# A diffusion transformer block on one core: a first chunk of four tiles of scale features, a new order of the head, and half tiles of the scores in pairs

## The chip, the core and the metric

The kernel runs on one core of one Trainium2 chip. The core has a matrix engine (TensorE, in the profile PE for its matmuls and PEld for its weight loads), a vector engine (DVE), a scalar engine (ACT), a general one (POOL) and a queue engine (SP) that issues most transfers. Matmuls take their operands from the on-chip memory SBUF (128 partitions) and write to PSUM, an accumulator memory of eight banks, each of 512 columns in float32 on 128 partitions. DVE and ACT read PSUM and write SBUF. The engines run their own instruction streams and wait for each other through semaphores.

The metric is the time of one execution in microseconds (us), as the device measures it; lower is better.

## What is computed

`x` holds two images (B = 2) of 256 tokens with 1152 features; `c` is one conditioning vector for each image. Everything is bfloat16 at the boundary.

```python
B, N, D = (2, 256, 1152); F = 4 * D
H = 2; Dh = D // H
mod = (_silu(c) @ w_mod).reshape(B, 6, 1, D)
shift_a, scale_a, gate_a, shift_m, scale_m, gate_m = [mod[:, i] for i in range(6)]
h = _layernorm(x, axis=-1) * (1 + scale_a) + shift_a
qkv = (h @ wqkv).reshape(B, N, 3, H, Dh)
q, k, v = qkv[:, :, 0], qkv[:, :, 1], qkv[:, :, 2]
attn = _softmax(jnp.einsum('bqhd,bkhd->bhqk', q, k) * Dh ** (-0.5), axis=-1)
a = jnp.einsum('bhqk,bkhd->bqhd', attn, v).reshape(B, N, D) @ wo
x = x + gate_a * a
h2 = _layernorm(x, axis=-1) * (1 + scale_m) + shift_m
m = _gelu(h2 @ w_fc1) @ w_fc2
return x + gate_m * m
```

1152 features are nine tiles of 128. A head has 576 features, which is four and a half tiles; so the fifth tile of Q (index 4) and of K (index 13 in the common buffer) belongs with its partitions 0 to 63 to head 0 and with its partitions 64 to 127 to head 1.

## The kernel before

**Planner.** The kernel records its work as units on the five engines, with the memory regions that each instruction reads and writes; a list scheduler then fixes an order for every engine and puts in the semaphore waits. TensorE and SP keep the order in which the units are recorded. DVE and ACT start with a list written out by hand (`S.first`) and go on by priority. Dependences in SBUF are by byte ranges. In PSUM they are by bank: an instruction of DVE or ACT waits for the last matmul of every TensorE unit that wrote the bank, for earlier accesses to the same bank by the other of the two engines, and a TensorE unit that writes a bank anew waits for all that read it before.

**Head.** The first transfers are `c` (issued from ACT), then, on SP's queue in this order: the two images of `x`; the scale columns of `w_mod` for the first `KC` = 5 feature tiles, in three pieces of three row blocks each (`ld_sc0_*`, WSC); the K weights of row blocks 0 to 4 (WK); the scale columns of the last four tiles in three pieces; the K weights of row blocks 5 to 8; the shift columns (WSH). Later come the Q weights (WQ), which use the place of WSC and whose loads wait until TensorE has read the row block of WSC that they overwrite.

While these arrive, TensorE runs matmuls without use (`warm`, identity times zeros `Q4B`, 512 columns) and turns `c` by a transpose. The layer norm's statistics of the four token tiles are shared between DVE (tiles 1 and 2: `bn_*`, `aggr_*`, `veps_*`) and ACT (tiles 0 and 3: `sq_*`, `sum_*`, then `nvar_*`, `veps_*` on DVE); POOL takes the inverse root, DVE writes the normalised tile `xn_t`. `xn_T(t)` transposes a token tile in nine matmuls of 128 columns into banks 4, 5, 6 for image 0 and 6, 4, 5 for image 1 (`XB`): feature tiles 0 to 3 in the first of these banks, 4 to 7 in the second, 8 in the third. `mod_kt` makes the scale features with matmuls of two columns into bank 7; `sc1a` (line 783, DVE) adds 1.

`hk(kt, b)` (line 792 on DVE, line 790 on ACT) multiplies feature tile `kt` of image `b` by its scale and writes it to `HK`. For the tiles of the first chunk it reads the transposed tile straight from PSUM; the others are first copied to SBUF by ACT (`xn_T_copy`, line 681), and scaled from there when the second chunk of scale features is known.

K is accumulated in pairs of output tiles (`k_pair`), each in one bank: image 0 in banks 0 to 3, image 1 in banks 5, 4, 6 (its fourth pair comes later, in bank 1). A pair takes two matmuls of 256 columns for each feature tile. Before, TensorE's order is: 15 warming matmuls, `xn_T(1)`, piece 0 of the scale features, one warming matmul, `xn_T(0)`, piece 1, two warming ones, piece 2, three warming ones; then the first five feature tiles of K of image 0 with `xn_T(2)` and `xn_T(3)` after the second and third of them; the first pair of image 1 with five tiles; all of the second chunk of scale features (36 matmuls); the second and third pair of image 1; and then the remaining feature tiles for both images. The contribution of the shift to K is left out, as it adds the same to all scores of a query, and shift is added (`hx`) only for Q and V.

**Q and scores.** Six tiles of Q are accumulated side by side in six banks, then moved to `QK` by ACT and DVE in turn (`qk_evac`). Tiles 6, 7 and 8 follow one by one (`proj`). `s_and_softmax(b, h)` computes the scores of one image and head, two blocks of 128 queries by 256 keys side by side in one bank (`s_bank`), over five chunks of features (`head_chunks`). The shared fifth tile of Q is stored twice: `QK[:, 4]` with zeros in partitions 64 to 127 (memset `z4a`) for head 0, and `Q4B` with zeros in partitions 0 to 63 for head 1. So both heads take a full matmul of 128 rows for it. DVE takes the row maximum, ACT the exponentials, DVE normalises. Between the scores stand the V projections; then come the transposed probabilities, the modulation rows, attention times V, the output projection, the second layer norm and the MLP, none of which the diff touches.

Where four small matmuls fill the four column groups of the array (`quad_mm`, for shift and for the modulation rows), a `tile_position` names the place; in the kernel before that is the only use of it.

Of the kernel before, what the change touches and what calls it, by code (L numbers as in the profile page):

```python
# [500 lines left out]
KT = 9  # L501
# [5 lines left out]
CH = 384  # L507
NCH = 3
F0 = 8
KC = 5  # L510
KG = 6


def c_mm(n):
    return max(n / 2.4 + 2.5, 27.0)
# [26 lines left out]
def build_kernel(nc, x, c, wqkv, wo, w_mod, w_fc1, w_fc2, out):  # L542
    S = Sched()
# [4 lines left out]
    with (  # L548
# [42 lines left out]
        WQ = wmat(O_A, D)  # L591
# [78 lines left out]
        def dve(cost, fn, reads, writes, name):  # L670
            return S.op("dve", cost, fn, reads=reads, writes=writes, name=name)
# [88 lines left out]
        def xn_T(t):  # L760
            b = t // 2
            S.unit("pe", KT * c_mm(128), "xnT_%d" % t)
            for kt in range(KT):
                tr(ps16(XB[b][kt // 4], (kt % 4) * 256 + (t % 2) * 128, 128), XN[:, t, kt * 128:(kt + 1) * 128], IDENT)

        def xn_T_copy(b, k0, k1, eng):
            src = ps16(XB[b][k0 // 4], (k0 % 4) * 256, (k1 - k0) * 256).rearrange("p (k t) -> p k t", k=k1 - k0)
            copy_on(eng, HX[:, k0:k1, b * 256:(b + 1) * 256], src, (k1 - k0) * 256, True, "xnT_cp%d_%d" % (b, k0))

        def warm(n, tag):  # L770
            for i in range(n):
                S.unit("pe", 215.0, "warm_%s_%d" % (tag, i))
                mm(ps32(2), IDENT, Q4B, True, True)

        def mod_kt(W, kt, col0, name, fs=(0, 9)):
            S.unit("pe", (fs[1] - fs[0]) * 27.0, name)
            for f in range(*fs):
                mm(ps32(7, col0 + f * 2, 2), W[:, kt, f * 128:(f + 1) * 128], ST[:, kt:18:9], kt == 0 and f == fs[0], kt == KT - 1,
                   skip_group_check=True)
# [6 lines left out]
        def hk(kt, b, eng="dve"):  # L786
            dst, s1 = HK[:, kt, b * 256:(b + 1) * 256], SC1A[:, kt * 2 + b:kt * 2 + b + 1]
            src = ps16(XB[b][kt // 4], (kt % 4) * 256, 256) if kt < KC else HX[:, kt, b * 256:(b + 1) * 256]
            if eng == "act":
                act(c_act(256, 1), lambda e: e.activation(out=dst, in_=src, func=ACTF.Copy, scale=s1), [src, s1], [dst], "hk_%d_%d" % (kt, b))  # L790
                return
            dve(256 if kt < KC else 200, lambda e: e.tensor_scalar(out=dst, in0=src, scalar1=s1, scalar2=None, op0=ALU.mult),  # L792
                [src, s1], [dst], "hk_%d_%d" % (kt, b))
# [10 lines left out]
        def k_pair(kts, i, b, bank=None):  # L804
            S.unit("pe", 2 * len(kts) * c_mm(256), "k%d_%d_%d" % (b, i, kts[0]))
            bank = KB[b][i] if bank is None else bank
            if kts[0] == 0:
                for kt in kts:
                    for half in range(2):
                        k_mm((kt,), 2 * i + half, b, bank, half)  # L810
            else:
                for half in range(2):
                    k_mm(kts, 2 * i + half, b, bank, half)
            if kts[-1] == KT - 1:
                eng = "act" if ev_rr[0] % 2 == 0 else "dve"
                ev_rr[0] += 1
                copy_on(eng, QK[:, 9 + 2 * i:11 + 2 * i, b * 256:(b + 1) * 256], ps32(bank).rearrange("p (j t) -> p j t", j=2), 512, False,
                        "k_ev%d_%d" % (b, i))

        warm(15, "b")  # L820
        xn_T(1)
        for kt in range(0, 3):
            mod_kt(WSC, kt, 0, "sca_%d" % kt, (0, KC))
        warm(1, "c")
        xn_T(0)
        for kt in range(3, 6):
            mod_kt(WSC, kt, 0, "sca_%d" % kt, (0, KC))
        warm(2, "d")
        for kt in range(6, 9):
            mod_kt(WSC, kt, 0, "sca_%d" % kt, (0, KC))  # L830
        warm(3, "e")
        sc1a(0, KC)
        for kt in range(KC):
            hk(kt, 0, "act" if kt in (2, 4) else "dve")
        xn_T_copy(0, 8, 9, "act")
        xn_T_copy(0, 5, 8, "act")
        for kt in range(KC):
            for i in range(4):
                k_pair((kt,), i, 0)
            if kt == 1:  # L840
                xn_T(2)
            if kt == 2:
                xn_T(3)
                xn_T_copy(1, 8, 9, "act")
                xn_T_copy(1, 5, 8, "act")
        for kt in range(KC):
            hk(kt, 1, "act" if kt == 2 else "dve")
        k_pair(range(KC), 0, 1)
        for kt in range(KT):
            mod_kt(WSC, kt, 0, "scb_%d" % kt, (KC, KT))  # L850
        sc1a(KC, KT)
        for kt in range(KC, KT):
            for b in range(2):
                hk(kt, b)
        k_pair(range(KC), 1, 1)
        k_pair(range(KC), 2, 1)
        for kt in range(KT):
            dma(WQ[:, kt, :], wqkv_v[:, kt, 0:D], P * D * 2, "ld_wq%d" % kt, run=2304)
        for kt in range(KC, KT - 2):
# [5 lines left out]
                k_pair((KT - 2, KT - 1), i, b)  # L865

        def qk_evac(j, bank):
            if j == 4:
                for eng, dst, src in (("act", QK[0:64, 4, :], psum[0:64, bank * 512:bank * 512 + 512]),
                                      ("dve", Q4B[64:128, :], psum[64:128, bank * 512:bank * 512 + 512])):  # L870
                    copy_on(eng, dst, src, 512, False, "qk_ev4" + eng)
                return
            copy_on("act" if ev_rr[0] % 2 == 0 else "dve", QK[:, j, :], ps32(bank), 512, False, "qk_ev%d" % j)
            ev_rr[0] += 1

        def proj(W, j, dst_j, H, bank):
# [1 line left out]
            for kt in range(KT):  # L878
                mm(ps32(bank), W[:, kt, j * 128:(j + 1) * 128], H[:, kt, :], kt == 0, kt == KT - 1)
            qk_evac(dst_j, bank)  # L880

        dve(330, lambda e: e.memset(QK[64:128, 4, :], 0.0), [], [QK[64:128, 4, :]], "z4a")

        def quads(w, g0, g1, q):
            return w.rearrange("p (g q c) -> p g q c", q=4, c=32)[:, g0:g1, q, :]
# [16 lines left out]
        for kt in range(KT):  # L902
            for b in range(2):
# [5 lines left out]
                else:  # L909
# [5 lines left out]

        S.first = {
# [5 lines left out]
        }  # L922


        head_chunks = {0: [(0, 9), (1, 10), (2, 11), (3, 12), (4, 13)], 1: [(-1, 13), (5, 14), (6, 15), (7, 16), (8, 17)]}
        s_bank = {(0, 0): 4, (1, 0): 5, (0, 1): 6, (1, 1): 3}

        def s_and_softmax(b, h):
            idx = b * 2 + h
            bank = s_bank[(b, h)]  # L930
            S.unit("pe", 10 * c_mm(256), "S_%d_%d" % (b, h))
            ch = head_chunks[h]
            for jq in range(2):
                for ci, (gq, gk) in enumerate(ch):
                    q0 = b * 256 + jq * 128
                    l = Q4B[:, q0:q0 + 128] if gq < 0 else QK[:, gq, q0:q0 + 128]
                    mm(ps32(bank, jq * 256, 256), l, QK[:, gk, b * 256:(b + 1) * 256], ci == 0, ci == len(ch) - 1)
            s3 = ps32(bank).rearrange("p (j k) -> p j k", j=2)
            mx, nb, rsum, ri, pp = MX[:, idx, :], NB[:, idx, :], RS[:, idx, :], RI[:, idx, :], PP[idx]
            dve(c_dve_psum32(512), lambda e: e.tensor_reduce(out=mx, in_=s3, axis=AX.X, op=ALU.max), [s3], [mx], "smax_%d" % idx)  # L940
            dve(165, lambda e: e.tensor_scalar(out=nb, in0=mx, scalar1=-SCALE, scalar2=None, op0=ALU.mult), [mx], [nb], "snb_%d" % idx)
            for jq in range(2):
                o, i_, bb, aa = pp[:, jq, :], ps32(bank, jq * 256, 256), nb[:, jq:jq + 1], rsum[:, jq:jq + 1]
                act(c_act(256, 1) + 200, lambda e, o=o, i_=i_, bb=bb, aa=aa: e.activation(out=o, in_=i_, func=ACTF.Exp, scale=SCALE, bias=bb, accum_out=aa),  # L944
                    [i_, bb], [o, aa], "sexp_%d_%d" % (idx, jq))
            dve(165, lambda e: e.reciprocal(out=ri, in_=rsum), [rsum], [ri], "sri_%d" % idx)
            rib = ri.unsqueeze(2).broadcast_to([P, 2, 256])
            dve(c_dve_tt16(512), lambda e: e.tensor_tensor(out=pp, in0=pp, in1=rib, op=ALU.mult), [pp, ri], [pp], "spn_%d" % idx)
# [157 lines left out]
        for j in range(KG):  # L1106
            qk_evac(j, qb[j])
        proj(WQ, 6, 6, HX, 0)
        s_and_softmax(0, 0)
        proj(WQ, 7, 7, HX, 1)  # L1110
        s_and_softmax(1, 0)
        proj(WQ, 8, 8, HX, 2)
        v_proj(0, 0)
        s_and_softmax(0, 1)
        v_proj(0, 1)
# [122 lines left out]
```

## Time and profile before

| | us |
|---|---|
| median of three runs | 246.71 (246.60 to 246.84) |
| the profiled execution | 246.34 |
| span of its records | 244.6 |
| TensorE matmul busy | 239.6 (98%) |
| ACT, DVE busy | 63.7, 99.3 |
| HBM read, mean over the span | 50.14 MB, 210 GB/s with the writes |

The span starts with the first record and ends with the last; the 1.7 us between it and the execution's time lie around it. "Busy" of PE counts each matmul with its passage through the array, so overlapping ones fill the time, and a busy PE is not necessarily at its peak rate. The time line and the chain give start, length and engine of instructions, with runs of the same instruction merged (`x15`), and in brackets the idle time before it with what ended it. `L686` is the helper that records every matmul and `L689` the one for transposes. Times are counted from the start of the span.

### The profile page before, as it was taken

How to read it: one execution, taken by the hardware profiler on the slowest of the kernel's cores; microseconds unless marked ns; L12 is line 12 of the kernel's file. 1: busy time of each engine (PE TensorE's matmuls, PEld its weight loads, DVE VectorE, ACT ScalarE, POOL GpSimd, SP SyncE). 2: the span in 40 equal slices, each digit the busy share in tenths (PEclk: the TensorE clock that was granted, in tenths of full speed). 3: DMA queues.
4: the chain of work that ended last, by engine and by line, in shares of the span. 5: the costliest groups of instructions: out<-in, count | busy, mean ns of one | idle time of the engine just before them, and what ended most of it. 6: DMA issues, size and time to landing. Idle time of an engine off the chain costs nothing.

```text
span 244.6 us, 3987 instructions
## 1 busy us (share of the span) xinstructions
PE 239.6 (98%) x1731; PEld 147.0 (60%) x1731; DVE 99.3 (41%) x206; ACT 63.7 (26%) x129; POOL 21.4 (9%) x37
## 2 busy tenths in 40 slices
PE   6999999999999999999999999999999999999995
PEld 2588844566657756798544444444566565665675
DVE  3743350555322779869999600000012222111112
ACT  5730340344311306983322333222000000000000
POOL 1400000000021275600000110000000000000000
PEclk9999999999999999999999999999999999999999
DMA  6999999999994999969943589200000000000000
GB/s 230 376 370 394 387 368 407 418 425 403 385 327 124 356 387 392 391 199 398 352 123 105 184 249 390 89 0 3 0 16 16 19 16 16 19 16 16 27 24 16
DMA packets 28875, 51.57 MB, mean 211 GB/s; under 512 B 1587, under 2 KB 15675, under 8 KB 28859
## 3 DMA queue, kind: packets, MB, share of 16 engines
q1 hardware_dynamic: 28384, 50.14, 56.9%
q0 software_dynamic: 448, 1.19, 1.7%
q8 instruction: 13, 0.21, 0.4%
q14 instruction: 3, 0.02, 0.0%
q10 hardware_dynamic: 27, 0.00, 0.0%
HBM read 50.14 MB, written 1.19 MB: 210 GB/s over the span
## 4 chain that ended last, share of the span: by engine, by line
PE 93%; DMA 3%; ACT 1%; SPq 1%; DVE 0%; issue 0%
PE psum L686 91%; DMA arena<-in_w_mod_dram 3%; PE psum L689 2%; ACT arena L1088 1%; SPq L667 1%; ACT arena L1070 1%; DVE arena L792 0%; DVE arena L1180 0%; DVE arena L1181 0%; DVE arena L783 0%
## 5 line engine op out<-in xcount | busy, mean ns | idle before, releaser
L686 PE MATMUL psum<-arena 128*128 128x384 bf16 (+9 forms) x1642 | 236.1, 312 | 1.8 <-POOL arena L709 1.4
L686 PEld LDWEIGHTS psum<-arena 128*128 128x128 bf16 (+1 forms) x1642 | 141.5, 97 | 91.7 <-issue 3.1
L1180 DVE TENSOR_TENSOR arena<-psum,arena 128x384 f32<-128x384 f32 (+3 forms) x14 | 7.0, 500 | 89.4 <-PE psum L686 89.4
L1098 ACT ACTIVATE arena<-psum 128x512 bf16<-128x512 f32 (+1 forms) x44 | 22.5, 522 | 42.6 <-PE psum L686 42.6
L681 ACT ACTIVATE arena<-psum 128x512 bf16<-128x512 f32 (+7 forms) x29 | 15.3, 550 | 34.9 <-PE psum L686 32.5
L683 DVE CAST arena<-psum 128x512 bf16<-128x512 f32 (+3 forms) x21 | 13.0, 627 | 26.5 <-PE psum L686 26.3
L999 DVE SCALAR_TENSOR_TENSOR arena<-arena 128x1152 f32<-128x1152 bf16 x16 | 21.3, 1409 | 0.0
L1065 POOL TENSOR_TENSOR arena<-arena 128x384 f32<-128x384 f32 x12 | 10.9, 912 | 13.3 <-DVE arena L1064 12.2
L667 POOL DMA_DIRECT2D dit_scratch<-arena x4 | 2.6, 662 | 94.5 <-ACT arena L681 59.2
L731 DVE BATCH_NORM_STATS2 arena<-arena 128x6 f32<-128x384 f32 (+1 forms) x18 | 9.5, 549 | 0.6 <-DMA arena<-in_x_dram 0.6
L689 PE MATMUL psum<-arena 128*128 128x128 bf16 (+1 forms) x89 | 7.3, 219 | 0.7 <-DMA arena<-in_c_dram 0.5
L1070 ACT ACTIVATE arena<-arena 128x1152 bf16<-128x1152 f32 x4 | 5.4, 1353 | 9.5 <-DVE arena L1069 9.5
L689 PEld LDWEIGHTS psum<-arena 128*128 128x128 bf16 (+1 forms) x89 | 5.9, 98 | 3.2 <-DMA arena<-in_c_dram 1.4
L1064 DVE TENSOR_TENSOR arena<-psum,arena 128x384 f32<-128x384 f32 x12 | 6.6, 548 | 3.2 <-PE psum L686 3.0
L1181 DVE TENSOR_TENSOR arena<-arena 128x384 bf16<-128x384 f32 (+3 forms) x14 | 7.0, 502 | 0.5
L1088 ACT ACTIVATE arena<-psum,arena 128x128 bf16<-128x128 bf16 x16 | 6.1, 460 | 3.2 <-PE psum L689 2.5
L1085 DVE TENSOR_SCALAR arena<-psum,arena 128x128 bf16<-128x128 bf16 x20 | 5.5, 335 | 2.0 <-PE psum L689 1.8
L944 ACT ACTIVATE arena<-psum,arena 128x256 bf16<-128x256 f32 x8 | 3.7, 470 | 6.9 <-PE psum L686 5.4
L735 POOL TENSOR_TENSOR arena<-arena 128x1 f32<-128x1 f32 x6 | 3.3, 553 | 5.5 <-DVE arena L734 5.5
L792 DVE TENSOR_SCALAR arena<-psum,arena 128x256 bf16<-128x256 bf16 x7 | 2.4, 349 | 2.7 <-PE psum L689 1.4
L940 DVE TENSOR_REDUCE arena<-psum 128x2 f32<-128x512 f32 x4 | 2.8, 689 | 1.5 <-PE psum L686 1.5
L907 ACT ACTIVATE arena<-arena 128x256 bf16<-128x256 bf16 x6 | 2.5, 495 | 3.3 <-DVE arena L901 3.3
(47 smaller groups left out, 43.4 us busy)
## 6 DMA issues: line engine op xcount, KB each, us to landing
arena<-in_w_mod_dram SPq DMA_DIRECT2D x4, 2592.0 KB, 19.5
arena<-in_w_fc_dram SPq DMA_DIRECT2D x9, 1152.0 KB, 7.9
arena<-in_w_fc_dram SPq DMA_DIRECT2D x4, 2592.0 KB, 17.4
arena<-in_wqkv_dram SPq DMA_DIRECT2D x18, 288.0 KB, 10.0
arena<-in_w_mod_dram SPq DMA_DIRECT2D x3, 864.0 KB, 12.6
arena<-in_wqkv_dram SPq DMA_DIRECT2D x1, 2592.0 KB, 10.4
arena<-in_wo_dram SPq DMA_DIRECT2D x1, 2592.0 KB, 32.9
arena<-in_w_mod_dram SPq DMA_DIRECT2D x3, 480.0 KB, 7.4
```

The costliest lines, as they stand in the source:

```text
L681: act(c_act(n), lambda e: e.activation(out=dst, in_=src, func=ACTF.Copy), [src], [dst], name)
L683: dve(c_dve_psum16(n) if psum16 else c_dve_psum32(n), lambda e: e.tensor_copy(dst, src), [src], [dst], name)
L686: S.instr(lambda e: e.matmul(o, lhsT=l, rhs=r, start=st, stop=sp, **kw), reads=[l, r], writes=[o])
L689: S.instr(lambda e: e.transpose(o, i_, idn), reads=[i_, idn], writes=[o])
L731: dve(550, lambda e, s=s, o=o: e.bn_stats(out=o, in_=s), [s], [o], "bn_%s_%d" % (tag, ci))
L999: u = dve(1300, lambda e, o=o, w=w, s1=s1: e.scalar_tensor_tensor(out=o, in0=w, scalar=s1, in1=o, op0=ALU.mult, op1=ALU.add), [w, s1, o], ...
L1065: S.op("pool", 930, lambda e, xs=xs, x1c=x1c: e.tensor_tensor(out=x1c, in0=x1c, in1=xs, op=ALU.add), reads=[x1c, xs], writes=[x1c], name=" ...
L1070: act(1344, lambda e: e.activation(out=xn2, in_=x1, func=ACTF.Identity, scale=rs, bias=nm), [x1, rs, nm], [xn2], "xn2_%d" % t)
L1088: act(440, lambda e, o=o, dst=dst, s1=s1, s2=s2: e.activation(out=dst, in_=o, func=ACTF.Identity, scale=s1, bias=s2), [o, s1, s2], [dst], ...
L1098: act(c_act(ntok), lambda e: e.activation(out=dst, in_=o, func=ACTF.Gelu_apprx_tanh), [o], [dst], "gelu_%d_%d" % (f, tok0))
L1180: dve(c_dve_psum32(w), lambda e, o=o, gm=gm, t1=t1: e.tensor_tensor(out=t1, in0=o, in1=gm, op=ALU.mult), [o, gm], [t1], "fc2_t1_%d_%d" % ( ...
L1181: dve(c_dve_32(w), lambda e, t1=t1, x1c=x1c, ost=ost: e.tensor_tensor(out=ost, in0=t1, in1=x1c, op=ALU.add), [t1, x1c], [ost], "fc2_out_%d ...
```

## The change

- `KC` becomes 4: the first chunk of scale columns has four feature tiles (rows of 1024 bytes in the transfers), the second five (rows of 1280 bytes). The K weights of row block 4 are now loaded after the second chunk. The copies to SBUF now start at feature tile 4 (1024 columns and 256 columns).
- TensorE's order in the head: 11 warming matmuls, piece 0 of the scale features, two warming ones, piece 1, one warming one, `xn_T(1)`, piece 2, `xn_T(0)`, two warming ones; K of image 0 for feature tiles 0 to 2; `xn_T(2)`, `xn_T(3)`; K of image 0 for tile 3; first pair of image 1 with four tiles; row blocks 0 to 2 of the second chunk of scale features; second pair; row blocks 3 to 8; third pair.
- The written lists for DVE and ACT follow: part of the statistics of tile 2 and those of tile 3 come after the first scaled tile; tiles 1 and 2 of image 0 and tile 1 of image 1 are scaled on ACT.
- The zeroed copies of Q's fifth tile go, with the memset `z4a`; its eviction is one instruction like the others, so the alternation of engines shifts by one for the evictions after it. `Q4B` remains as the operand of the warming matmuls.
- `s_halves` computes the fifth tile's part of all scores: for each image and block of queries a matmul on partitions 0 to 63 into head 0's bank and one on partitions 64 to 127 into head 1's bank, with `tile_position` (0, 0) and (64, 0). It stands before the first scores, opens their banks, and the scores then add their four full chunks.
- The order after Q's sixth tile: projections 6 and 7, the half tiles, scores (image 0, head 0), projection 8, scores (1, 0), then as before.

```diff
-KC = 5
+KC = 4
...
-        warm(15, "b")
-        xn_T(1)
+        warm(11, "b")
         for kt in range(0, 3):
             mod_kt(WSC, kt, 0, "sca_%d" % kt, (0, KC))
-        warm(1, "c")
-        xn_T(0)
+        warm(2, "c")
         for kt in range(3, 6):
             mod_kt(WSC, kt, 0, "sca_%d" % kt, (0, KC))
-        warm(2, "d")
+        warm(1, "d")
+        xn_T(1)
         for kt in range(6, 9):
             mod_kt(WSC, kt, 0, "sca_%d" % kt, (0, KC))
-        warm(3, "e")
+        xn_T(0)
+        warm(2, "e")
         sc1a(0, KC)
         for kt in range(KC):
-            hk(kt, 0, "act" if kt in (2, 4) else "dve")
+            hk(kt, 0, "act" if kt in (1, 2) else "dve")
         xn_T_copy(0, 8, 9, "act")
-        xn_T_copy(0, 5, 8, "act")
+        xn_T_copy(0, KC, 8, "act")
         for kt in range(KC):
+            if kt == 3:
+                xn_T(2)
+                xn_T(3)
+                xn_T_copy(1, 8, 9, "act")
+                xn_T_copy(1, KC, 8, "act")
             for i in range(4):
                 k_pair((kt,), i, 0)
-            if kt == 1:
-                xn_T(2)
-            if kt == 2:
-                xn_T(3)
-                xn_T_copy(1, 8, 9, "act")
-                xn_T_copy(1, 5, 8, "act")
         for kt in range(KC):
-            hk(kt, 1, "act" if kt == 2 else "dve")
-        k_pair(range(KC), 0, 1)
-        for kt in range(KT):
-            mod_kt(WSC, kt, 0, "scb_%d" % kt, (KC, KT))
+            hk(kt, 1, "act" if kt == 1 else "dve")
+        for i in range(3):
+            k_pair(range(KC), i, 1)
+            if i < 2:
+                for kt in range(3 * i, 3 * i + 3):
+                    mod_kt(WSC, kt, 0, "scb_%d" % kt, (KC, KT))
+            if i == 1:
+                for kt in range(6, 9):
+                    mod_kt(WSC, kt, 0, "scb_%d" % kt, (KC, KT))
         sc1a(KC, KT)
...
-        k_pair(range(KC), 1, 1)
-        k_pair(range(KC), 2, 1)
...
         def qk_evac(j, bank):
-            if j == 4:
...
-                return
...
-        dve(330, lambda e: e.memset(QK[64:128, 4, :], 0.0), [], [QK[64:128, 4, :]], "z4a")
...
             "dve": [...
-                    "xn_1", "xn_0", "bn_ln1_2_1", "bn_ln1_2_2", "aggr_ln1_2", "veps_ln1_2", "nvar_ln1_3", "veps_ln1_3",
-                    "sc1a_0", "hk_0_0", "xn_2", "hk_1_0", "xn_3", "hk_3_0", "z4a", "hk_0_1", "hk_1_1", "hk_3_1", "hk_4_1", "sc1a_5"],
-            "act": ["ld_c", "c_tanh", "sq_ln1_0", "sum_ln1_0", "sq_ln1_3", "sum_ln1_3", "xnT_cp0_8", "xnT_cp0_5", "hk_2_0", "hk_4_0",
-                    "hk_2_1", "xnT_cp1_8", "xnT_cp1_5"],
+                    "xn_1", "xn_0", "bn_ln1_2_1", "sc1a_0", "hk_0_0", "bn_ln1_2_2", "aggr_ln1_2", "veps_ln1_2", "nvar_ln1_3", "veps_ln1_3",
+                    "hk_3_0", "xn_2", "xn_3", "hk_0_1", "hk_2_1", "hk_3_1", "sc1a_4"],
+            "act": ["ld_c", "c_tanh", "sq_ln1_0", "sum_ln1_0", "sq_ln1_3", "sum_ln1_3", "hk_1_0", "hk_2_0", "xnT_cp0_8", "xnT_cp0_4",
+                    "hk_1_1", "xnT_cp1_8", "xnT_cp1_4"],
...
-        head_chunks = {0: [(0, 9), (1, 10), (2, 11), (3, 12), (4, 13)], 1: [(-1, 13), (5, 14), (6, 15), (7, 16), (8, 17)]}
+        head_chunks = {0: [(0, 9), (1, 10), (2, 11), (3, 12)], 1: [(5, 14), (6, 15), (7, 16), (8, 17)]}
...
+        def s_halves():
+            S.unit("pe", 4 * c_mm(256) + 100.0, "S_halves")
+            for b in range(2):
+                for jq in range(2):
+                    for h in range(2):
+                        r = slice(64 * h, 64 * h + 64)
+                        q0 = b * 256 + jq * 128
+                        mm(ps32(s_bank[(b, h)], jq * 256, 256), QK[r, 4, q0:q0 + 128], QK[r, 13, b * 256:(b + 1) * 256],
+                           jq == 0, False, skip_group_check=True, tile_position=(64 * h, 0))
...
-                    l = Q4B[:, q0:q0 + 128] if gq < 0 else QK[:, gq, q0:q0 + 128]
-                    mm(ps32(bank, jq * 256, 256), l, QK[:, gk, b * 256:(b + 1) * 256], ci == 0, ci == len(ch) - 1)
+                    mm(ps32(bank, jq * 256, 256), QK[:, gq, q0:q0 + 128], QK[:, gk, b * 256:(b + 1) * 256], False, ci == len(ch) - 1,
+                       skip_group_check=True)
...
         proj(WQ, 6, 6, HX, 0)
+        proj(WQ, 7, 7, HX, 1)
+        s_halves()
         s_and_softmax(0, 0)
-        proj(WQ, 7, 7, HX, 1)
+        proj(WQ, 8, 8, HX, 2)
         s_and_softmax(1, 0)
-        proj(WQ, 8, 8, HX, 2)
         v_proj(0, 0)
```

More of the change, by code (lines that the diff above doesn't have):

```diff
@@ L867, in qk_evac @@
         def qk_evac(j, bank):
-            if j == 4:
-                for eng, dst, src in (("act", QK[0:64, 4, :], psum[0:64, bank * 512:bank * 512 + 512]),
-                                      ("dve", Q4B[64:128, :], psum[64:128, bank * 512:bank * 512 + 512])):
-                    copy_on(eng, dst, src, 512, False, "qk_ev4" + eng)
-                return
             copy_on("act" if ev_rr[0] % 2 == 0 else "dve", QK[:, j, :], ps32(bank), 512, False, "qk_ev%d" % j)
@@ L930, in s_and_softmax @@
             bank = s_bank[(b, h)]
-            S.unit("pe", 10 * c_mm(256), "S_%d_%d" % (b, h))
+            S.unit("pe", 8 * c_mm(256), "S_%d_%d" % (b, h))
             ch = head_chunks[h]
```

## The prediction

> **What bounds the kernel now.** I read the page's busy shares and chain first, then the chain in order of time, then the time line of the head, and last single records of TensorE (start to start).
>
> ```profile
> span 244.6 us, 3987 instructions
> PE 239.6 (98%) x1731; PEld 147.0 (60%) x1731; DVE 99.3 (41%) x206; ACT 63.7 (26%) x129; POOL 21.4 (9%) x37
> PE 93%; DMA 3%; ACT 1%; SPq 1%; DVE 0%; issue 0%
> ...
> 2.69 8.13 DMA arena<-in_w_mod_dram
> 10.83 0.05 issue
> 10.87 0.67 PE psum L686 x15
> ```
>
> Until 10.83 the end hangs on the first chunk of scale weights; afterwards on TensorE. From 12.18 to the end the matmul records stand back to back except at eight places, together 0.87 us: 0.06 and 0.13 before the second chunk of scale features, four gaps of 0.093 to 0.096 where a stretch with four column tiles begins or ends, and 0.25 and 0.06 near 98 and 107. So two things count: when K begins, and how much matmul time and how many gaps follow.
>
> ```profile
> 11.57 0.17 DVE L783 TENSOR_SCALAR arena<-psum 128x10 f32<-128x10 f32 x1 [0.92 <-PE psum L686]
> 11.77 0.35 DVE L792 TENSOR_SCALAR arena<-psum,arena 128x256 bf16<-128x256 bf16 x1
> 12.17 1.64 PEld L686 LDWEIGHTS psum<-arena 128*128 128x128 bf16 x16 [0.58 <-DVE arena L792]
> ...
> 14.44 1.04 PE L686 MATMUL psum<-arena 128*128 128x256 bf16 x8
> ...
> 15.31 0.67 PE L689 MATMUL psum<-arena 128*128 128x128 bf16 x9
> ...
> 16.02 0.61 DVE L792 TENSOR_SCALAR arena<-psum,arena 128x256 bf16<-128x256 bf16 x2 [1.42 <-PE psum L689]
> 16.72 0.47 ACT L790 ACTIVATE arena<-psum,arena 128x256 bf16<-128x256 bf16 x1 [2.98 <-PE psum L686]
> 17.10 1.08 ACT L681 ACTIVATE arena<-psum 128x256 bf16<-128x256 bf16 x2
> ```
>
> The reader should see the relay: scale features, 1+scale (L783), first scaled tile (L792), first K matmul. Eight K matmuls span 1.04 including the last one's 0.27 of pipeline, so one costs 0.109; a transpose by the same reading 0.056. Single records give a two-column scale matmul 0.0266 and a 512-column one 0.216.
>
> **The first chunk, four tiles.** The trace has the landing of each transfer. The three present ones (480 KB, rows of 1280 bytes) land at 8.28, 9.57 and 10.83, 1.27 apart; those of the second chunk (384 KB, rows of 1024 bytes) at 15.90, 17.04 and 18.08, 1.09 apart.
>
> ```profile
> arena<-in_w_mod_dram SPq DMA_DIRECT2D x3, 480.0 KB, 7.4
> arena<-in_x_dram SPq DMA_DIRECT2D x2, 576.0 KB, 4.2
> arena<-in_w_mod_dram SPq DMA_DIRECT2D x3, 384.0 KB, 10.0
> ```
>
> By these spacings three transfers save 3 x 0.18 = 0.54. By the queue's rate (352 GB/s at 7 to 8 us with the long rows, 350 at 15 to 16 with the short) 1.475 MB takes 4.20 and 1.18 MB 3.36: 0.84. Landings follow the slowest of 16 engines, so I take 0.65, nearer the spacing: the last piece at 10.18. Rows of 1024 bytes carry less per packet here (48 ns against 55 for 1280, where a fifth less would be 44). The Trainium skill (DMA: Bandwidth & Descriptors, Specifications) puts line rate at 512 bytes and up; by it a transfer would take four fifths, 1.02, the saving would be 0.76 and the sum 0.1 better. The trace's packets disagree mildly.
>
> **K's start.** Formerly both images' tile transposes were done while waiting; now xn_T(1) stands between pieces two and three, and xn_T(0) behind the third. Piece two lands at 9.14; its 12 matmuls end at 9.50, a warming one at 9.71, xn_T(1) at 10.21: just when piece three is usable (10.22). Its 12 matmuls (0.32) end at 10.54, xn_T(0) at 11.04, its last transpose starting at 10.99. In the rows a scaled tile starts 0.257 after the last transpose's start (15.758, 16.015), hence 11.25; 1+scale is ready before. From L792 to K it is 0.407 (11.772, 12.179): K at 11.65. The two warming matmuls end at 11.47, hidden. **Gain 0.53**, not 0.65: the first scaled tile starts 1.07 after the landing in place of 0.94 (11.77 - 10.83), as xn_T(0) now ends after 1+scale. K's first weights land at 11.74 - 0.65 = 11.09, before they are needed. If the cover of xn_T(1) goes too (piece two late), at most 0.5 more.
>
> **The scaled tiles and the copies.** Different engines on one PSUM bank are made to wait for each other in program order: image 0's scaled tiles run DVE 11.25, ACT 11.64 and 12.01, so ready at 12.11 and 12.48, needed at 12.52 and 13.40. Hidden. The 1024-column copy has no row; 768 columns take 0.81 and 256 take 0.38, so between 0.81 and 1.62, by the slope 1.02. It ends at about 13.4, and its bank is wanted by xn_T(2) at 14.27. The statistics moved behind the first scaled tile on DVE (bn 0.55, aggregate 0.24, three small ones of 0.15 to 0.21, POOL 0.57 twice, xn 0.57 twice) give xn_2 at 13.8 and xn_3 at 14.4, wanted at 14.27 and 14.77. Hidden by 24 K matmuls (2.62).
>
> **A wait that replaces two.** xn_T(2) and xn_T(3) run from 14.27 to 15.27, and only eight matmuls follow (to 16.15) before image 1's first pair, which writes bank 5, from which ACT must first copy the ninth tile. That copy stands on ACT behind a scaled tile, and that one waits for DVE's: DVE 15.47 to 15.82, ACT from 15.92, the copy 16.29 to 16.67, and as in the rows (17.473, 17.617) the matmul 0.144 later: 16.81. Stall 0.66, against 0.06 + 0.13 now: **loss 0.47**. Everything later on TensorE moves by it. In the kernel before, sixteen matmuls covered the same relay. The bounds of this stall are 0 and 0.8.
>
> **Second chunk.** Nine more two-column matmuls in the dense part: 9 x 0.0266 = **loss 0.24**. It lands at 18.08 - 0.65 - 0.75 (one K weight now behind it) + 3 x 0.18 = 17.2, wanted from 17.7. The K weight moved behind it lands by 18.9, wanted at 20.6. The last pair (0.87) covers the second 1+scale and the first tile scaled from it (0.17 + 0.28 and two handovers). The Q loads, each of which waits until TensorE has read the scale weights in its place, are issued at 18 to 20 as now, on SP's queue behind the shift weights that land until 28.6: hidden by 8 us. In the sum: all five tiles of all seven pairs done at 22.17 against 21.99, **0.18 later**.
>
> **Scores.** Before, 40 matmuls of 256 columns; eight of them with a zeroed half (0.872). After, 32 and eight half matmuls, two on the two halves of the rows. No row shows row halves. The nearest are the four column tiles:
>
> ```profile
> L686 PE MATMUL psum<-arena 128*2 128x288 bf16 x36 | 1.3, 286 | 0.0
> ...
> 30.16 0.96 PEld L686 LDWEIGHTS psum<-arena 128*2 128x2 bf16 x36 [0.21 <-issue]
> ...
> 31.36 14.57 PEld L686 LDWEIGHTS psum<-arena 128*128 128x128 bf16 x69 [0.25 <-issue]
> ```
>
> 36 matmuls from 30.16 to 31.37 less a gap of 0.096 are 1.11, nine times 0.123: four run in one's time, and each change of tiling costs 0.095. Lower end: pairs without a change's cost, 0.436, gain 0.44. Upper end: in turn, each with its own change, 8 x 0.204 = 1.63, loss 0.76. I take pairs with two changes, 0.436 + 0.19 = 0.63, **gain 0.24**, as the column rows show that. The Trainium skill (TensorE: Matmul & The Clock Gate, Measured speedup vs the span model) adds 4 ns per further tile, which would make it 0.02 less. Moving the third Q projection behind the first scores leaves the work; the softmax of the last scores starts as late as now, its transposes have 1.46 of V ahead. The evictions of Q's fifth tile become one of 0.6 to 0.7 instead of two halves, and later ones change engine: TensorE stands 1.9 us of projection ahead of their readers.
>
> **Sum.** +0.18 - 0.24 = -0.06 against the profiled execution (246.34, span 244.6): 246.28. The runs shown have a median of 246.71, 0.37 above; against it 246.65. What this kernel's measurement can tell from no change is about 0.2%, 0.49 us.
>
> **Rivals.**
> - *The stall at bank 5 is covered.* ACT would take the copy as early as image 1's transposes end, and K of image 1 begins at 16.2. For: the same relay costs only 0.06 now. Against: the copy's place behind a tile that waits for DVE. Then -0.53 + 0.24 - 0.13 - 0.24 = -0.66: 246.05. With the landing's upper end 245.9. Chance 0.32.
> - *Row halves do not overlap* (the other side). The eight take turns, with the array emptied between: 0.87 + 0.19 to 1.63, so +0.18 plus 0.19 to 0.76: 247.1 to 247.65. It decides the sign against the 0.2% once the eight take more than 1.2 us. For: no row shows it. Against: the column tiles overlap fully. Chance 0.14.
> - *The clock gate closes again.* The array reached full clock at 6.01, after 3 us of dense matmuls; after the change eleven warming ones end near 6.9, and until K TensorE is idle or transposing much of the time. K's first matmuls would take 0.213: up to 1.7 us over one closed stretch of 3.4, 247.2 to 248.4. Against: the longest idle piece would be 1.1, and later gaps in the records close nothing. The Trainium skill (same page, Part 4) says transposes do not count as activity; no run here shows it. Chance 0.06.
> - *The second chunk or its K weight lands over a microsecond late*, as one slow engine made the load after it land 1.54 behind instead of 0.75: +0.5, 247.2. Chance 0.04.
> - *My sum*: 0.44, between 246.2 and 247.1.
>
> Faster by over 0.2%: 0.32; within: 0.44; slower: 0.14 + 0.06 + 0.04 = 0.24. The likeliest is no telling difference, 246.6. The range runs from 245.8 (the covered stall with a good landing) to 247.4 (halves in turn with part of the changes); outside lie about a tenth on each side.
>
> **What would show it.** The last of the first chunk landing between 10.0 and 10.3; first K matmul at 11.5 to 11.8; a gap of about 0.66 before image 1's first pair, released by ACT; all five tiles done near 22.2; the eight half matmuls spanning 0.44 with 0.095 on either side. Wrong would be: no gap there, halves 0.109 apart each, or K matmuls 0.213 apart.

## The result and the profile after

| | before | changed |
|---|---|---|
| median of 22 executions each | 246.59 | 247.04 |
| lowest, highest | 245.93, 246.91 | 246.51, 248.79 |
| profiled execution, its span | 246.34, 244.6 | 247.78, 246.0 |

The ratio is 1.0030, with a 95% interval from 1.0019 to 1.0042: slower by 0.3%, where no telling difference was forecast. The spread says more than the median. The execution's mean granted clock of TensorE is 1.00 (0.999 at least) in 13 of the 22, which lie at 246.51 to 247.34 with a median of 246.72; it is 0.992 or 0.993 in the other nine, which lie at 247.78 to 248.79 with a median of 248.2. The profiled execution is one of the nine.

The page of the changed kernel, the lines that answer to those shown before, and from its slices the matmul row and the clock row (tenths, 6.15 us a slice):

```profile
span 246.0 us, 3969 instructions
PE   7789999999999999999999999999999999999995
PEclk9799999999999999999999999999999999999999
PE 93%; DMA 3%; ACT 1%; issue 1%; SPq 0%; DVE 0%
```

The second and third digit of PE are 7 and 8, where the kernel before has 9s, and the second digit of PEclk is a 7. The changed kernel's windows, cut at the records of the granted clock (time, length, busy time and count of PE, PEld, DVE, ACT and POOL in this order, clock, share and rate of the transfers):

```profile
2.70:6.11 3.41, 3.41 (x9) 1.19 (x9) 1.85 (x6) 1.69 (x5) 0.19 (x1) 1.00 0.94 344
6.11:9.52 3.41, 2.00 (x28) 0.90 (x27) 2.73 (x8) 3.38 (x6) 1.39 (x2) 1.00 0.98 307
9.52:12.94 3.42, 3.20 (x40) 2.59 (x39) 0.68 (x4) 0.07 (x2) 0.00 (x0) 0.50 1.03 380
```

The clock opened at 6.11, and 3.41 us later it was taken back to half for another 3.41. The clock column shows 1.00 also where no record stands, as in the first line: until 6.11 the 512-column matmuls start 0.427 apart, after it 0.215. The closed stretch holds the transposes of `xn_T(1)` and `xn_T(0)` and the scale features of the last piece; a transpose takes 0.107 there in place of 0.056, and K begins at 13.01, 0.07 after the clock came back. In the kernel before, TensorE was busy for 3.37 of the window that answers to the middle line, and the clock stayed:

```profile
6.01:9.42 3.41, 3.37 (x40) 2.08 (x39) 2.73 (x9) 3.38 (x6) 1.39 (x2) 1.00 1.02 357
```

For the steps of the prediction, an execution of the changed kernel with full clock is needed; a later group of executions (e11_changed_again) left one. Its chain in order of time, and its time line around image 1's first pair and the second chunk:

```profile
2.88 7.86 DMA arena<-in_w_mod_dram
10.73 0.05 issue
10.78 0.47 PE psum L686 x12
11.24 0.52 PE psum L689 x9
11.77 0.43 PE psum L686 x2
12.20 0.10 issue
12.30 2.78 PE psum L686 x24
```

```profile
16.13 0.35 DVE L792 TENSOR_SCALAR arena<-psum,arena 128x256 bf16<-128x256 bf16 x1 [1.15 <-PE psum L689]
16.57 0.47 ACT L790 ACTIVATE arena<-psum,arena 128x256 bf16<-128x256 bf16 x1 [2.29 <-PE psum L686]
16.95 1.29 ACT L681 ACTIVATE arena<-psum 128x256 bf16<-128x256 bf16 x2
17.08 0.61 DVE L792 TENSOR_SCALAR arena<-psum,arena 128x256 bf16<-128x256 bf16 x2 [0.60 <-ACT arena L790]
17.43 3.72 PEld L686 LDWEIGHTS psum<-arena 128*128 128x128 bf16 x69 [0.76 <-DVE arena L792]
...
20.83 0.17 DVE L783 TENSOR_SCALAR arena<-psum 128x10 f32<-128x10 f32 x1 [3.14 <-PE psum L686]
21.03 1.27 DVE L792 TENSOR_SCALAR arena<-arena 128x256 bf16<-128x256 bf16 x6
21.37 0.88 PEld L686 LDWEIGHTS psum<-arena 128*128 128x128 bf16 x9 [0.21 <-DVE arena L792]
```

The last piece lands at 10.73, K begins at 12.30. The relay of image 1 is there as worked out: DVE, then ACT, then ACT's copy of the ninth tile (the first of the two at 16.95), and only then the pair, at 17.46. The bracket names DVE, whose semaphore the weight load also takes. But DVE's first tile, the one that it needs, had long ended; that copy ended at 17.32, the wait for ACT's semaphore at 17.41, and the load started 0.02 later. A last gap of 0.10 stands at 21.37, where the first tile of the next group is scaled too late.

The half tiles, in the profiled execution with the slow start (weight loads):

```profile
50.59 0.33 PEld L686 LDWEIGHTS psum<-arena 64*128 64x128 bf16 x8 [0.42 <-issue]
50.70 0.60 ACT L681 ACTIVATE arena<-psum 128x512 bf16<-128x512 f32 x1 [2.31 <-PE psum L686]
51.13 0.88 PEld L686 LDWEIGHTS psum<-arena 128*128 128x128 bf16 x9 [0.21 <-issue]
```

From the first half matmul (50.595) to the first full one (51.139) it is 0.544, and 0.095 more go before: 0.64 for all, 0.63 forecast.

### The profile page after: what moved, and what is told of

Same layout as the page of the kernel before. It is cut to its first block, busy times and chain, and to the rows that moved or that the text cites. A ratio compares the mean times of both kernels' runs of the same rounds, so it can differ in the third digit from the quotient of the medians.

```text
span 246.0 us, 3969 instructions
## 1 busy us (share of the span) xinstructions
PE 239.1 (97%) x1716; PEld 147.0 (60%) x1726; DVE 98.5 (40%) x205; ACT 63.3 (26%) x128; POOL 21.6 (9%) x37
## 4 chain that ended last, share of the span: by engine, by line
PE 93%; DMA 3%; ACT 1%; issue 1%; SPq 0%; DVE 0%
PE psum L686 91%; DMA arena<-in_w_mod_dram 3%; PE psum L689 2%; ACT arena L1093 1%; ACT arena L1075 1%; SPq L667 0%; ACT arena L790 0%; DVE arena L792 0%; DVE arena L1186 0%; DVE arena L1187 0%
## 5 line engine op out<-in xcount | busy, mean ns | idle before, releaser
L686 PE MATMUL psum<-arena 128*128 128x384 bf16 (+10 forms) x1627 | 234.5, 312 | 4.1 <-POOL arena L709 1.4
L686 PEld LDWEIGHTS psum<-arena 128*128 128x128 bf16 (+2 forms) x1637 | 141.0, 97 | 93.8 <-issue 4.5
L681 ACT ACTIVATE arena<-psum 128x512 bf16<-128x512 f32 (+6 forms) x28 | 15.2, 566 | 40.5 <-PE psum L686 38.5
L683 DVE CAST arena<-psum 128x512 bf16<-128x512 f32 (+2 forms) x21 | 13.0, 627 | 26.4 <-PE psum L686 26.2
L689 PE MATMUL psum<-arena 128*128 128x128 bf16 (+1 forms) x89 | 8.1, 238 | 0.2
L689 PEld LDWEIGHTS psum<-arena 128*128 128x128 bf16 (+1 forms) x89 | 6.6, 107 | 2.5 <-DMA arena<-in_c_dram 1.0
L790 ACT ACTIVATE arena<-psum,arena 128x256 bf16<-128x256 bf16 x3 | 1.3, 472 | 5.7 <-PE psum L689 3.4
```

The lines of the kernel that those rows point to most:

```text
L681: act(c_act(n), lambda e: e.activation(out=dst, in_=src, func=ACTF.Copy), [src], [dst], name)
L683: dve(c_dve_psum16(n) if psum16 else c_dve_psum32(n), lambda e: e.tensor_copy(dst, src), [src], [dst], name)
L686: S.instr(lambda e: e.matmul(o, lhsT=l, rhs=r, start=st, stop=sp, **kw), reads=[l, r], writes=[o])
L689: S.instr(lambda e: e.transpose(o, i_, idn), reads=[i_, idn], writes=[o])
```

## The experiments

Kernels tried together ran on one chip beside the kernel before, whose median there stands with each result (246.55 to 247.10). Comparisons are within a group; between groups they go by the difference to the kernel before.

**Half tiles and the head, each alone.** e2_halves is the kernel before with the diff's part from `qk_evac` to the order of the projections:

```diff
...
+        proj(WQ, 7, 7, HX, 1)
+        s_halves()
         s_and_softmax(0, 0)
-        proj(WQ, 7, 7, HX, 1)
+        proj(WQ, 8, 8, HX, 2)
...
```

> The kernel before with the half tiles of the scores and the new order of Q's last projections alone; the head stays. By the prediction's term for the scores: 0.24 less than the kernel before, 246.3, granted clock 1.00 throughout, the eight half matmuls spanning 0.44 with 0.09 on either side. Rival H (halves in turn): 0.2 to 0.8 more, 246.8 to 247.4. If theory G holds, no execution loses clock here.

Measured: 246.33 (11 executions, 246.07 to 246.68) against 246.66; ratio 0.9989, interval 0.9981 to 0.9998; clock at least 0.999 in all. The gain is 0.33, in the trace the eight take 0.64 in place of 0.87. Halves in turn are out: the two of a pair start 0.004 apart.

e3_head is the changed kernel without that part, with the scores as before:

> The changed head with the scores as before (zeroed copies of Q's fifth tile, 40 full matmuls). Theory G: both kinds of executions as in the changed kernel, each 0.24 longer: some 246.9 with full clock, some 248.3 with a clock of 0.992, the latter in a third to a half of them; median near 247.3. Rival H: if the half tiles cost time, this one is shorter than the changed kernel.

Measured: 247.92 (six executions) against 246.66; ratio 1.0057, interval 1.0036 to 1.0079. Three at full clock, 247.24 to 247.56, three at 0.993, 248.28 to 248.91. So the loss lies in the head, and both kinds of executions come. But each lies 0.4 to 0.5 over its expectation (medians 247.43 and 248.70 against 246.9 and 248.3). The trace shows why (time line from 22 to 23.5 us):

```profile
21.89 0.17 DVE L783 TENSOR_SCALAR arena<-psum 128x10 f32<-128x10 f32 x1 [3.14 <-PE psum L686]
22.17 0.27 DVE L884 MEMSET arena<- 64x256 uint32 x1
22.47 1.26 DVE L792 TENSOR_SCALAR arena<-arena 128x256 bf16<-128x256 bf16 x6
```

With the scores as before the memset `z4a` comes back, and it is no longer in DVE's written list; here it falls between 1+scale and the first tile of the second chunk. TensorE waits 0.48 there, in place of 0.10 in the changed kernel. So of the 0.77 with full clock, by three executions, some 0.38 belong to this version alone and about 0.4 to the changed head. The median falls between the groups, and six executions do not place it well.

**The clock.** e8_starved is the kernel before with ten warming matmuls taken away:

```diff
-        warm(15, "b")
+        warm(11, "b")
...
-        warm(1, "c")
-        warm(2, "d")
-        warm(3, "e")
```

> The kernel before with 11 first warming matmuls in place of 15 and without the six later ones; nothing else differs, and none of the ten taken away is on the way of data. Theory G: the clock falls to 0.992 in some executions (a quarter or more), each 1 to 1.6 longer; the others stay at 246.6. Rival T: transposes count as activity, so the clock stays at 1.00 and the time at 246.6.

Measured: 248.71 (six executions, 247.95 to 249.46) against 246.55; ratio 1.0091, interval 1.0072 to 1.0111. All six have a clock of 0.985 to 0.993. Its windows:

```profile
3.46:6.88 3.42, 3.42 (x10) 1.05 (x8) 2.34 (x6) 2.50 (x5) 0.70 (x2) 1.00 0.96 330
6.88:10.29 3.41, 2.39 (x50) 1.92 (x48) 2.82 (x9) 3.09 (x7) 0.88 (x2) 1.00 1.01 344
10.29:13.70 3.41, 2.21 (x23) 1.67 (x24) 2.33 (x8) 1.25 (x3) 1.06 (x2) 0.50 1.03 390
13.70:17.12 3.42, 3.42 (x23) 2.69 (x21) 0.27 (x1) 0.00 (x0) 0.00 (x0) 0.50 1.11 366
```

Nothing but matmuls without use was removed, the data land when they did (the last piece at 10.70), and the kernel loses 2.16. All executions lost clock, where a quarter or more was expected, each 1 to 1.6 longer. So a starved TensorE costs time by its clock alone. The window before the closing is busy for 2.39 us: 0.32 are the end of the last warming matmul, the rest transposes and two-column matmuls. The next is busy for 2.21, and the clock stays at half for one more; K's matmuls run 0.213 apart from 12.06 until it is over. Three of the six executions have the clock of one closed stretch (0.993, 1.4 to 1.8 over the kernel before), three that of two (0.985 and 0.986, 2.5 to 2.9 over).

In e3_head's trace a window busy for 2.46 us, with nine transposes and three whole warming matmuls, was followed by a closed one (10.66 to 14.08).

Three kernels add warming matmuls to the changed one. e1_filled puts eight into all the waits (15, 4, 3, 2 in place of 11, 2, 1, 2), e5_warm15 four and e12_warm13 two at the start alone:

```diff
-        warm(11, "b")
+        warm(15, "b")
```

> The changed kernel with 24 warming matmuls in the head in place of 16 (15, 4, 3 and 2 in place of 11, 2, 1 and 2), placed in the waits for the three pieces. Theory G (clock gate): the changed kernel's lost 0.3% come from executions in which the array returns to half clock from about 9.5 to 12.9 us, since TensorE is idle for much of 6.1 to 9.5; here the granted clock is 1.00 in every execution and the median is 246.5 to 246.8, level with the kernel before. Rival L (late landing): K begins late as the first chunk lands at 10.8, as before; the half clock hides behind that wait; the times stay at 246.6 to 248.8 with a median near 247.0.

Measured: 247.39 (eight executions) against 246.66; ratio 1.0034, interval 1.0022 to 1.0046; clock at least 0.999 in all. The clock came as expected, the time did not: in its trace the last piece lands at 10.15, but K begins at 12.12, hardly before the 12.18 of the kernel before, for the three warming matmuls ahead of xn_T(1) now stand in the way. It is a first sign that the clock is not all of the loss.

> The changed kernel with 15 first warming matmuls as in the kernel before, nothing else changed; these four more end before the first piece lands (7.8) and delay nothing. Theory G (the gate closes when TensorE streams too little over 6.1 to 9.5; 0.85 us of warming columns there were too few, 1.9 enough): clock 1.00 in every execution, median 246.6 to 246.85, the level of the changed kernel's executions with full clock (246.72). Rival T (the gate counts something else, as that transposes come late): executions at 0.993 and about 248.2 remain in a third or more.

Measured: 247.09 (nine executions, 246.75 to 247.34) against 246.55; ratio 1.0025, interval 1.0015 to 1.0034; clock at least 0.999 in all. Again the clock as expected and the time not: without any closing, the median stays 0.54 over the kernel before. The changed kernel's 13 executions with full clock (0.13 over) had been taken for its level, and may be only the lucky ones. The next two were made for that.

> The changed kernel itself once more, beside the next one on one chip, as the executions of e5_warm15 with full clock had a median of 247.09 and those of the changed kernel 246.72. Theory G with phase: the window of the clock's monitor has its own phase; the changed kernel has full clock only where the phase is kind, and these executions stand 0.1 to 0.3 over the kernel before, the others 1.3 to 1.7 over it. Rival: e5's extra 0.37 is of its chip; then the two kernels' executions with full clock are level here.

Measured: 247.43 (12 executions) against 247.01; ratio 1.0021, interval 1.0001 to 1.0040. Nine with full clock, 246.42 to 247.59, median 247.26 (0.25 over the kernel before); three at 0.993, 248.25 to 248.54.

> The changed kernel with 13 first warming matmuls, between the changed kernel's 11 and e5's 15. Theory G: fewer executions at 0.993 than in e11_changed_again on the same chip (none to one in five, against a third to a half); the executions with full clock have a wider spread than there, 246.6 to 247.3, since phases that closed the gate before now only cost time with slow warming matmuls. Rival: the same share closes, as warming before 7 us is not what the window misses.

Measured: 247.25 (12 executions, 246.74 to 247.80) against 247.01; ratio 1.0009, interval 0.9995 to 1.0023; none with a closed gate. None of 12 against three of 12 beside them is too few to tell by itself; with e1, e4 and e5 it is none of 40 executions with two or more warming matmuls added, against 12 of 34 without. The spread did not widen as I had expected. That a late opening costs something of its own shows in a trace: in e9_five_relay below the clock opened only at 8.96, the first 13 of the 15 warming matmuls took 0.40 to 0.43 each, the last began after 9, the transposes queued behind them, and K began at 13.06, 2.19 after the last piece (in e2_halves, with the same order, 1.35).

**The stall at bank 5.** e4_copy_first is e1_filled with this:

```diff
-            hk(kt, 1, "act" if kt == 1 else "dve")
+            hk(kt, 1, "dve")
...
-                    "hk_3_0", "xn_2", "xn_3", "hk_0_1", "hk_2_1", "hk_3_1", "sc1a_4"],
+                    "hk_3_0", "xn_2", "xn_3", "hk_0_1", "hk_1_1", "hk_2_1", "hk_3_1", "sc1a_4"],
...
-                    "hk_1_1", "xnT_cp1_8", "xnT_cp1_4"],
+                    "xnT_cp1_8", "xnT_cp1_4"],
```

> The kernel of e1_filled, with all four tiles of image 1 scaled on DVE and ACT's copy of the ninth tile first in its list. By the prediction's step the stall of 0.66 before image 1's first pair goes nearly wholly (TensorE ready at 16.2, the bank free at 16.0): 0.5 to 0.65 less than e1_filled, 245.9 to 246.2. Rival: the stall moves to the next pair's bank or to the second chunk's landing, and the time falls by less than 0.2.

Measured: 246.62 (11 executions) against 246.66, ratio 1.0001, interval 0.9992 to 1.0009, so 0.77 less than e1_filled beside it. The fall is larger than expected, the level higher, as e1_filled itself lay higher. Its time line at the same place:

```profile
15.78 2.96 PE L686 MATMUL psum<-arena 128*128 128x256 bf16 x37
15.98 1.30 ACT L681 ACTIVATE arena<-psum 128x256 bf16<-128x256 bf16 x2 [1.84 <-PE psum L689]
15.98 1.13 DVE L792 TENSOR_SCALAR arena<-psum,arena 128x256 bf16<-128x256 bf16 x4 [1.15 <-PE psum L689]
```

ACT's copies and DVE's four tiles start together at 15.98, and K's matmuls run on without a gap. The stall was worth its whole length.

**Bytes or rows in the first chunk.** e7_rows512 splits each of the first three transfers into two of 512-byte rows (the same bytes, 2304 rows):

```diff
+                for c0, c1 in (((0, 256), (256, 512)) if ka == 0 else ((ka * P, kb * P),)):
+                    dma(WSC[:, k0:k0 + 3, c0:c1], wmod_v[:, k0:k0 + 3, D + c0:D + c1], 3 * P * (c1 - c0) * 2,
```

> The changed kernel with each of the three first transfers of scale columns split in two of 512-byte rows: the same bytes in twice the rows. If rows set the pace of the first chunk (as 1152 rows took about as long with 1024 bytes as with 1280), it lands 1.5 us or more later than the 10.15 to 10.8 seen, at 12 or after. If bytes set it: within 0.3 of that.

Measured in a single execution: the last piece lands at 10.33; the time is 246.62. Twice the rows cost nothing in it; rows do not set the pace.

**Mended versions.** e6_relay is the changed kernel with e4's edit, 14 first warming matmuls, and xn_T(1) and xn_T(0) in the waits after pieces 0 and 1:

```diff
-        warm(2, "c")
+        xn_T(1)
+        warm(1, "c")
...
-        warm(1, "d")
-        xn_T(1)
+        xn_T(0)
         for kt in range(6, 9):
             mod_kt(WSC, kt, 0, "sca_%d" % kt, (0, KC))
-        xn_T(0)
```

> The changed kernel with three of its steps mended: 14 first warming matmuls; xn_T(1) after piece 0 and xn_T(0) after piece 1, so that both run while data are awaited; image 1's tiles all scaled on DVE and the copy of the ninth tile first on ACT. By the measured terms: stall -0.66, K's start -0.15, clock 1.00 throughout: 245.9 to 246.2, below both kernels and below the half tiles alone (246.33). Rival: a new wait (first tile of the next group, second chunk's landing) takes the gain back and it stays at 246.3 to 246.6.

Measured: 246.20 (12 executions) against 246.55; ratio 0.9992, interval 0.9977 to 1.0007. Eleven with full clock, 245.78 to 246.69, and one at 0.993 with 247.96, where none was expected; it widens the interval.

> The kernel of e6_relay with two more warming matmuls (15 at first, one between xn_T(0) and piece 2). Theory G: no execution with a clock of 0.993 (one of twelve before); median 246.1 to 246.3, its worst execution under 247. Rival: the closing of the gate is not set by these windows; about one in ten stays at 248.

Measured: 246.58 (12 executions, 246.15 to 247.21) against 247.10 on that chip; ratio 0.9977, interval 0.9965 to 0.9990; clock at least 0.999 in all. It lies 0.52 under the kernel before, by an interval clear of 1; the changed kernel lay over it. Its median is over the 246.1 to 246.3 expected by about as much as the kernel before is over its own on this chip, and its worst execution is 0.21 over the expected 247.

> The kernel of e2_halves (five tiles in the first chunk, the head of before, half tiles of the scores) with image 1's tiles all scaled on DVE and ACT left to the two copies. The two gaps of 0.06 and 0.13 before and inside image 1's first pair should go: 0.15 to 0.2 less than e2_halves, 246.1 to 246.2, clock 1.00 throughout. If the four-tile chunk is worth something beside its waits, e10_relay_filled is below this one; if the 0.24 of additional small matmuls outweighs the 0.35 by which its last piece lands earlier, it is level or above.

Measured: 246.72 (12 executions) against 247.10; ratio 0.9987, interval 0.9973 to 1.0000. The two gaps are gone from its trace. By the difference to the kernel before it is 0.05 under e2_halves (0.38 and 0.33), where 0.15 to 0.2 were expected; two chips stand between them. e10 lies 0.14 below it, which the two intervals do not tell apart.

## Why the prediction was wrong, step by step

The forecast was -0.06 of a sum, and a chance of 0.06 for the clock's closing. Two things failed. That the median of 247.04 lies within the stated range is partly luck: it falls where two groups of executions meet, each for a reason that the sum did not have.

*The rival on the clock gate.* "Against: the longest idle piece would be 1.1, and later gaps in the records close nothing" was the wrong reading. It does not take an idle window: the window before the closing was busy for 2.00 of 3.41 us in the changed kernel, 2.39 in e8_starved, 2.46 in e3_head. The bound of its price was right (up to 1.7; 1.48 between the two medians). Its place was right in part. In the profile of the changed kernel no K matmul ran slow, so the sign named for it (K matmuls 0.213 apart) is missing: the closed stretch slowed the transposes, and K began 2.21 after the last piece in place of 1.57, a price of 0.64. In e3_head's, K began 2.15 after it and six steps of 0.21 between K matmuls followed, together 1.3. Its chance was wrong: it came in 12 of 34 executions of the changed kernel, in none of the 91 executions of the kernel before beside the experiments, and in six of six when only warming was taken from it. By the two groups of the first 22, closing makes up 0.56 of the mean (nine of 22 times 1.37 between the means 246.80 and 248.17), and pulls the median up to where the groups meet. Taking it away gave less: in the mean the changed kernel is 0.76 over the kernel before and e5_warm15 0.53, and on one chip e11 is 0.46 over it and e12_warm13 0.23. So 0.23 to 0.56 of the mean is the clock's, and how much is open.

*K's start, "Gain 0.53".* With full clock the changed kernel was still 0.13 (13 executions), 0.25 (nine) and, with 15 warming matmuls, 0.54 over the kernel before, not level. The term that is off most is the landing, "the last piece at 10.18". In the nine profiles of kernels with four tiles in rows of 1024 bytes it lands at 10.15 to 11.10, in the mean at 10.57; in the four with five tiles at 10.70 to 10.87, mean 10.80. So 0.23 was saved in the mean, not 0.65 and not even the 0.54 of the lower bound, and single landings differ by more than that. I had taken the spacing of transfers from a later stretch (1.09 between landings at 16 to 18 us); early the same rows came slower: over the nine profiles the first three landings are 1.30 apart in the mean, no closer than the 1.28 of the longer rows. From 7 to 8 us the queue of the changed kernel moved 292 GB/s, that of the kernel before 352. From the landing to K it took 1.57 (10.73 to 12.30) where 1.47 was forecast: the first scaled tile starts 1.08 after the landing, as forecast, but K follows it by 0.50 in place of 0.41. In the trace TensorE takes the wait for DVE first and that for the K weights (landed at 11.52) after it, in the kernel before the other way round; whether this order is the reason was not tried. The kernel before takes 1.35. Together, 0.23 less 0.22, the gain of 0.53 is nothing in the mean, and in the execution shown K begins 0.12 later than before. The rule that rows of 512 bytes already run at line rate (the Trainium skill, DMA: Bandwidth & Descriptors, Specifications) agrees with e7's 10.33; but the saving of 0.76 worked out from it was further off than mine.

*The wait that replaces two.* Right in place, releaser and size: 0.665 to 0.667 in every one of the traces that kept it (0.66 forecast), gone in those that reordered the relay, and worth 0.77 in time there.

*The second chunk.* Nine more matmuls took the 0.24. "The last pair covers the second 1+scale and the first tile scaled from it" was 0.10 short: the gap at 21.37.

*Scores.* Right: 0.64 against 0.63, pairs at the price of one and 0.095 for each change of tiling; in time 0.33 (interval of the ratio 0.9981 to 0.9998) against 0.24. What the Trainium skill says of it (TensorE: Matmul & The Clock Gate, Measured speedup vs the span model, 4 ns for a further tile) agrees with the trace, where the second of a pair starts 0.003 to 0.004 after the first.

*The sum, made again.* For the execution shown: K 0.12 later, the stall 0.667 in place of 0.183, 0.24, 0.10: 0.94 by the end of the first tiles. The trace has 22.92 in place of 21.99, which is 0.93. Less 0.23 for the scores this is 0.70; the spans differ by 0.7 (245.3 and 244.6). So between these two executions, both with full clock, nothing is missing. The medians there differ by only 0.25, as the profiled execution of the kernel before is a short one (246.34). The rival "the stall is covered" did not come, nor did late weights in any trace.

*What stays open.* Why the queue is slower from 5 to 9 us with shorter rows (512-byte rows moved 312 GB/s there, 1024-byte ones 292, 1280-byte ones 352, in one trace each). Nine of ten rows of the first chunk took 46 ns with 1024 bytes and 55 with 1280, but the means from 5 to 10 us are 53.8 and 60.0 in the traces of the two kernels: a few rows are slow in both. What the monitor counts: in e7 a window busy for 2.02 us stayed open, with more 512-column warming in it (1.44 us against 1.08 in the changed kernel's, counted from start to start at full clock), and in e6_relay one of 2.53 us. Whether the amount of work decides or its kind is not told apart. And why one chip shows more slow openings than another: the clock opened at 4.3 to 9.0 us in the profiles, and I did not control it.

## What to carry to other kernels

Matmuls that compute nothing may be holding the clock: before taking them away, or before moving useful work out of a wait, add up TensorE's busy time over each window of 3.4 us until the dense part begins, for several places of the window (here windows of 2.0 to 2.5 us were the doubtful ones), and read the granted clock of every execution, not of one profile. When a chunk is cut to start earlier, cut the work that covers the next relay as well in the sum: here the four-tile chunk left eight matmuls over a relay that had had sixteen. And take a transfer's pace from the same stretch of the same queue, not from a later one.

## What the runs showed of the hardware

The clock's records are 3.413 apart (6.111, 9.524, 12.938), and windows with 2.00, 2.39 and 2.46 us of TensorE time were followed by a closed one. The Trainium skill (TensorE: Matmul & The Clock Gate, What's actually happening, the table of states) gives one idle window of about 3.4 us as the condition for the way back to half clock. The period agrees, the condition, read as a window without work, does not. In e8_starved, transposes and two-column matmuls for 2.07 us, with 0.32 of warming before them, did not hold it. A transpose runs at the granted clock: 0.056 us at full, 0.107 at half.

Two matmuls on the two halves of the array's rows, writing two banks, ran in the time of one: eight of 256 columns in 0.544, of which 0.093 is the change back to the full array.
